# Batch 0's kv sums in one PSUM tile of two banks, and the last output tile in column groups of 320 and 192 instead of 384 and 128

## The chip, the cores and the metric

The kernel runs on one core of one Trainium2 chip. The metric is the device time of one execution in microseconds, the median of several. The time before was 279.4 us. The packed traces keep nanoseconds, while the views round events to 0.01 us and spans to 0.1 us; distances with three decimals below are taken from the packed traces.

## The reference, cut to what matters

```python
def _attn_ref(q, k, v):                      # batch 8, heads 8, sequence 576, head_dim 64
    q_s = softmax(q, axis=-1)                # exp, then divided by the sum over d
    k_s = softmax(k, axis=2)                 # exp, then divided by the sum over the sequence
    kv = np.einsum('bhsd,bhse->bhde', k_s, v)
    return np.einsum('bhsd,bhde->bhse', q_s, kv)

def _moe_ref(x, w_in, w_out):                # 4608 tokens, 512 -> 2048 -> 512
    h = x @ w_in
    g = gelu(h)
    return g @ w_out
```

The code is abridged. The attention output, regrouped by token, is `x`. The softmax of `k` needs no division before the product: the kernel appends a column of ones to `v`, so that the 65th column of kv is the sum, and divides afterwards.

## The kernel before

Nearly all of the time is the two large products (`h_mm`, `y_mm`) on TensorE. The change touches the two ends: the attention of batch 0, which must be done before the first `h_mm`, and the last output tile.

The heads are handled as four pairs (`hp`), two pairs to a half. `kv_mm` sums one half on TensorE, from `ek` (exp of k) and `v_aug` (v in bf16 with its column of ones); `kv_norm` divides it on VectorE into `kvc`, by way of the reciprocals `rec`; `x_mm` then multiplies by the transposed q (`qT`), and an evacuation copies the result to `xT`, the input of `h_mm`. PSUM is the buffer that the matmuls write, and it is divided into banks. Batch 0 has four PSUM banks for its four pairs, two of them from the pool `h`:

```python
def kv_tiles(b):
    if b == 0:
        p = [psum_h.tile([128, 512], FP32, tag="h", name="kv")[:, 0:256] for i in range(2)]
        ps = psum_a.tile([128, 4, 256], FP32, tag="a2", name="kv")   # two banks
        st[b]["kvall"] = ps[:, 0::2]
        p += [ps[:, 0, :], ps[:, 2, :]]
    else:
        ps = psum_a.tile([128, 4, 256], FP32, tag="a2", name="kv")
        st[b]["kvall"] = ps
        p = [ps[:, i, :] for i in place]
    st[b]["kv"] = p
place = [1, 2, 0, 3]

def kv_norm(b, half=None):
    # [cut: which slices; for b == 0 and half == 0 two parts of one pair each]
    for src, dst, m in parts:
        nc.vector.reciprocal(rec[:, 0:m], src[:, :, D])
        nc.vector.tensor_tensor(out=dst, in0=src[:, :, 0:D], in1=[cut: rec, broadcast], op=ALU.mult)

# batch 0, in program order
cast_v(0, 0, nc.scalar); cast_v(0, 1, nc.scalar)
tp_evac(0, 0)
cast_v(0, 2, nc.gpsimd); cast_v(0, 3, nc.gpsimd)
# [cut: two x tiles]
tp_mm(0, 1)                    # second half of the transposes of q
tp_evac(0, 1, "s")
x_tile(0, 2, psum_a, "a")
kv_mm(0, 0)
kv_norm(0, 0)
kv_mm(0, 1)
kv_norm(0, 1)
# [cut: casts of the first weights]
x_mm(0, 0)
x_evac(0, 0, "s"); x_evac(0, 1)
x_mm(0, 1)
x_evac(0, 2, "s"); x_evac(0, 3)
# [cut] then h_phase(0): the first h_mm
```

The last output tile of 128 rows is computed in two column groups, so that the first group's stores are under way while the second is summed:

```python
def y_last():
    for i, (c0, n) in enumerate(((0, 384), (384, 128))):
        ps = psum_y.tile([128, DM], FP32, tag="y")
        for t in range(NDF):                     # 16 matmuls of n columns
            nc.tensor.matmul(ps[:, 0:n], [cut: g], wo_bf[:, t, c0:c0 + n], [cut])
        nc.vector.tensor_copy(out=y_sb[:, 0:n], in_=ps[:, 0:n])
        # [cut] two stores of 64 rows, one issued by SyncE and one by ScalarE
```

The softmax here doesn't subtract the row's maximum and nothing guards it: scores larger than these inputs give would overflow.

Of the kernel before, what the change touches and what calls it, by code (L numbers as in the profile page):

```python
# [8 lines left out]
FP32 = mybir.dt.float32  # L9
# [7 lines left out]
def kernel(  # L17
# [35 lines left out]
    psum_h = ctx.enter_context(tc.tile_pool(name="psum_h", bufs=3, space=bass.MemoryType.PSUM))  # L53
    psum_y = ctx.enter_context(tc.tile_pool(name="psum_y", bufs=2, space=bass.MemoryType.PSUM))
    psum_a = ctx.enter_context(tc.tile_pool(name="psum_a", bufs=1, space=bass.MemoryType.PSUM))
# [12 lines left out]
    kvc = [singles.tile([128, HP, D], BF16, name=f"kvc{b}") for b in range(B)]  # L68
# [12 lines left out]
    st = [dict() for _ in range(B + 1)]  # L81
# [93 lines left out]
    def kv_tiles(b):  # L175


        if b == 0:
            p = [psum_h.tile([128, 512], FP32, tag="h", name="kv")[:, 0:256] for i in range(2)]
            ps = psum_a.tile([128, 4, 256], FP32, tag="a2", name="kv")  # L180
            st[b]["kvall"] = ps[:, 0::2]
            p += [ps[:, 0, :], ps[:, 2, :]]
        else:
            ps = psum_a.tile([128, 4, 256], FP32, tag="a2", name="kv")
            st[b]["kvall"] = ps
            p = [ps[:, i, :] for i in place]
        st[b]["kv"] = p

    place = [1, 2, 0, 3]

# [4 lines left out]
    def kv_mm(b, half):  # L195


        if "kv" not in st[b]:
            kv_tiles(b)
        for n in range(NS):  # L200
            for i in range(2):
                for hh in range(2):
                    hp = 2 * half + i
                    pr = slice(hh * 64, hh * 64 + 64)
                    c = slice((hh ^ i) * 64, (hh ^ i) * 64 + 64)
                    nc.tensor.matmul(  # L206
                        st[b]["kv"][hp][c, 0:D + 1], ek[b % 2][pr, hp, n, :],
                        v_aug[b % 2][pr, hp, n, 0:D + 1], start=(n == 0), stop=(n == NS - 1),
                    )

    def kv_norm(b, half=None):

        ps = st[b]["kvall"]
        if half is None:
            parts = [(ps, kvc[b], 4)]
        elif b == 0 and half == 0:
            parts = [(st[b]["kv"][hp].unsqueeze(1), kvc[b][:, hp:hp + 1], 1) for hp in range(2)]
        elif b == 0:
            parts = [(ps, kvc[b][:, 2:4], 2)]
        else:  # L220
            parts = [(ps[:, 1:3] if half == 0 else ps[:, 0::3], kvc[b][:, 2 * half:2 * half + 2], 2)]
        for src, dst, m in parts:
            rec = small.tile([128, 4], FP32, tag="reck")
            nc.vector.reciprocal(rec[:, 0:m], src[:, :, D])  # L224
            nc.vector.tensor_tensor(  # L225
                out=dst, in0=src[:, :, 0:D],
                in1=rec[:, 0:m].unsqueeze(2).to_broadcast([128, m, D]), op=ALU.mult,
            )

    def kv_step(b):  # L230
        kv_mm(b, 0)
        kv_mm(b, 1)
        kv_norm(b)
# [161 lines left out]
    def y_last():  # L395

        j = J - 1
        for i, (c0, n) in enumerate(((0, 384), (384, 128))):
            ps = psum_y.tile([128, DM], FP32, tag="y")
            for t in range(NDF):  # L400
                nc.tensor.matmul(  # L401
                    ps[:, 0:n], st[B]["g"][:, t, j * 128:(j + 1) * 128],
                    wo_bf[:, t, c0:c0 + n], start=(t == 0), stop=(t == NDF - 1),
                )
            y_sb = moe_sb.tile([128, DM], FP32, tag="y_sb")
            nc.vector.tensor_copy(out=y_sb[:, 0:n], in_=ps[:, 0:n])  # L406
            for b2 in range(2):
                r0 = (2 * j + b2) * S + M
                eng = nc.scalar if b2 else nc.sync
                eng.dma_start(  # L410
                    out=out[r0:r0 + R, c0:c0 + n], in_=y_sb[b2 * R:(b2 + 1) * R, 0:n]
                )

    def y_phase(c, ins):
        for j in range(J - 1 if c == B else J):
            ps = psum_y.tile([128, DM], FP32, tag="y")
            for t in range(NDF):
                y_mm(c, ps, j, t)
                for f in ins.get((j, t), []):
                    f()  # L420
            y_out(c, ps, j)
        if c == B:
            y_last()
# [117 lines left out]
# [5 lines that stand above are left out]
    for dm in range(NDM):  # L546
        cast_wi_dm(0, wi[0], dm, nc.gpsimd)
# [177 lines left out]
```

## Time and profile before

| event, from the timeline of before | us |
|---|---|
| first kv matmul (first half) | 11.55 |
| second kv half released | 12.55 |
| x matmuls of the second half start | 13.63 |
| first h matmul | 13.97 |
| first matmul of the last tile | 270.42 |
| end of the span | 277.5 |

From the first h matmul to the last tile TensorE has no gap to speak of: 256.45 us. This distance is 256.44 to 256.47 us in twelve of the thirteen traces in the fast state, so a kernel's span is the start (up to the first h matmul), plus 256.45, plus the tail (from the last tile on, 7.05 here: the span is 277.471 us before rounding). The profile lines stand in the prediction.

### The profile page before, as it was taken

How to read it: one execution, taken by the hardware profiler on the slowest of the kernel's cores; microseconds unless marked ns; L12 is line 12 of the kernel's file. 1: busy time of each engine (PE TensorE's matmuls, PEld its weight loads, DVE VectorE, ACT ScalarE, POOL GpSimd, SP SyncE). 2: the span in 40 equal slices, each digit the busy share in tenths (PEclk: the TensorE clock that was granted, in tenths of full speed). 3: DMA queues.
4: the chain of work that ended last, by engine and by line, in shares of the span. 5: the costliest groups of instructions: out<-in, count | busy, mean ns of one | idle time of the engine just before them, and what ended most of it. 6: DMA issues, size and time to landing. Idle time of an engine off the chain costs nothing.

```text
span 277.5 us, 4658 instructions
## 1 busy us (share of the span) xinstructions
PE 270.9 (98%) x1966; PEld 125.6 (45%) x1966; DVE 100.8 (36%) x154; ACT 158.9 (57%) x247; POOL 32.5 (12%) x26
## 2 busy tenths in 40 slices
PE   7799999999999999999999999999999999999995
PEld 3344454444444444444444444444444444444443
DVE  2876565319743540263008400751015200120012
ACT  4867686689377717791669246943683363126400
POOL 1520041002020310013000500050005000000000
PEclk9999999999999999999999999999999999999999
DMA  7999999974993249613981189117402500220033
GB/s 258 400 374 427 402 400 404 400 271 116 312 307 64 77 109 297 239 40 94 268 320 38 53 215 398 56 41 193 109 0 78 151 0 0 78 76 0 2 76 77
DMA packets 44980, 50.10 MB, mean 181 GB/s; under 512 B 20384, under 2 KB 29856, under 8 KB 44704
## 3 DMA queue, kind: packets, MB, share of 16 engines
q1 hardware_dynamic: 44560, 49.39, 53.5%
q10 hardware_dynamic: 400, 0.43, 0.5%
q8 instruction: 15, 0.25, 0.4%
q14 instruction: 5, 0.04, 0.1%
HBM read 36.70 MB, written 9.44 MB: 166 GB/s over the span
## 4 chain that ended last, share of the span: by engine, by line
PE 94%; DMA 4%; POOL 0%; DVE 0%; issue 0%; SPq 0%
PE ps L348 44%; PE ps L376 44%; DMA f<-in_v_dram 2%; PE kv L206 2%; PE ps L315 2%; DMA f<-in_q_dram 2%; PE ps L401 1%; PE pair L348 1%; POOL v_aug L169 0%; PE ps L320 0%; PE tp L279 0%; SPq L103 0%; DVE kvc L225 0%; DVE y_sb L406 0%; DVE rec L224 0%
## 5 line engine op out<-in xcount | busy, mean ns | idle before, releaser
L348 PE MATMUL ps<-xT,wi_bf 128*128 128x512 bf16 x568 | 124.9, 379 | 0.0
L376 PE MATMUL ps<-wo_bf,g 128*128 128x512 bf16 x560 | 124.1, 379 | 0.0
L354 ACT ACTIVATE g<-ps 128x512 bf16<-128x512 f32 x142 | 83.5, 598 | 66.8 <-PE ps L348 66.7
L348 PEld LDWEIGHTS <-wi_bf 128*128 128x128 bf16 x576 | 56.2, 98 | 68.0 <-issue 0.8
L376 PEld LDWEIGHTS <-g 128*128 128x128 bf16 x560 | 54.0, 98 | 64.6 <-issue 0.4
L384 DVE COPY y_sb<-ps 128x512 f32<-128x512 f32 x33 | 22.7, 687 | 81.0 <-PE ps L376 80.7
L245 POOL TENSOR_TENSOR e<-e,recq 128x2048 bf16<-128x2048 bf16 (+1 forms) x9 | 25.7, 2855 | 175.9 <-DVE recq L244 141.2
L169 DVE CAST v_aug<-f 128x576 bf16<-128x576 f32 x24 | 16.4, 746 | 48.3 <-DMA f<-in_v_dram 48.3
L243 DVE TENSOR_REDUCE qsum<-e 128x16 f32<-128x1024 bf16 (+1 forms) x13 | 21.1, 1622 | 13.7 <-ACT e L152 13.6
L341 ACT CAST xT<-ps 128x512 bf16<-128x512 f32 x18 | 9.9, 588 | 26.4 <-PE ps L315 15.9
L152 ACT ACTIVATE e<-f 128x512 bf16<-128x512 f32 (+1 forms) x42 | 20.5, 556 | 3.5 <-DMA f<-in_q_dram 3.5
L157 ACT ACTIVATE ek<-f 128x2304 bf16<-128x2304 f32 (+1 forms) x10 | 17.2, 1728 | 0.6 <-DMA f<-in_k_dram 0.5
L339 DVE CAST xT<-ps 128x512 bf16<-128x512 f32 x17 | 11.0, 687 | 17.1 <-PE ps L315 14.1
L79 ACT ACT_TABLE_LOAD x9 | 11.5, 1283 | 2.8 <-issue 2.7
L494 PE MATMUL ps<-zeros 128*128 128x512 f32 x14 | 8.0, 734 | 1.5 <-DVE zeros L520 1.5
L152 ACT ACT_TABLE_LOAD x7 | 9.0, 1283 | 0.1
L453 DVE CAST wi_bf<-w 128x512 bf16<-128x512 f32 x12 | 7.1, 621 | 1.8 <-DMA w<-in_moe_w_in_dram 1.4
L206 PEld LDWEIGHTS <-ek 64*64 64x64 bf16 x576 | 6.4, 105 | 2.2 <-issue 0.6
L206 PE MATMUL kv<-v_aug,ek 64*64 64x65 bf16 x576 | 6.8, 193 | 0.5 <-POOL v_aug L169 0.5
L487 DVE CAST wo_bf<-w 128x2048 bf16<-128x2048 f32 (+1 forms) x5 | 4.5, 907 | 6.1 <-DMA w<-in_moe_w_out_dram 6.1
L245 DVE TENSOR_TENSOR e<-e,recq 128x1024 bf16<-128x1024 bf16 x4 | 6.2, 1544 | 0.1
L315 PE MATMUL ps<-qT,kvc 64*64 64x512 bf16 x62 | 5.4, 390 | 0.3 <-DVE kvc L225 0.3
(40 smaller groups left out, 48.2 us busy)
## 6 DMA issues: line engine op xcount, KB each, us to landing
out_dram<-y_sb SPq DMA_DIRECT2D x32, 256.0 KB, 2.4
f<-in_k_dram SPq DMA_DIRECT2D x6, 1152.0 KB, 9.9
f<-in_v_dram SPq DMA_DIRECT2D x6, 1152.0 KB, 11.7
f<-in_q_dram SPq DMA_DIRECT2D x6, 1024.0 KB, 7.7
w<-in_moe_w_in_dram SPq DMA_DIRECT2D x6, 512.0 KB, 8.6
f<-in_v_dram SPq DMA_DIRECT2D x8, 288.0 KB, 6.5
f<-in_q_dram SPq DMA_DIRECT2D x4, 512.0 KB, 8.9
w<-in_moe_w_out_dram SPq DMA_DIRECT2D x2, 1024.0 KB, 11.4
```

The lines of the kernel that those rows point to most:

```text
L79: nc.scalar.activation(out=scr[:, 1:2], in_=scr[:, 0:1], func=func)
L152: nc.scalar.activation(out=dst[:, i], in_=src[:, u], func=AF.Exp)
L157: nc.scalar.activation(out=ek[b % 2][:, i:i + n], in_=st[b]["kf"][:, i:i + n].rearrange("p x (n d) -> p x n d", n=NS), func=AF.Exp,)
L169: eng.tensor_copy(out=o, in_=i)
L206: nc.tensor.matmul(st[b]["kv"][hp][c, 0:D + 1], ek[b % 2][pr, hp, n, :], v_aug[b % 2][pr, hp, n, 0:D + 1], start=(n == 0), stop=(n == NS - 1),
L243: nc.vector.reduce_sum(out=qsum, in_=eq[:, :, hs, :], axis=AX.X)
L245: eng.tensor_tensor(out=eq[:, :, hs, :], in0=eq[:, :, hs, :], in1=recq.unsqueeze(3).to_broadcast([128, J, w, D]), op=ALU.mult,)
L339: nc.vector.tensor_copy(out=st[b]["xT"][:, hp, :], in_=ps)
L348: nc.tensor.matmul(ps, wi_bf[:, dm, t * 128:(t + 1) * 128], st[c]["xT"][:, dm, :], start=(dm == 0), stop=(dm == NDM - 1),)
L354: nc.scalar.activation(out=st[c]["g"][:, t, :], in_=ps, func=AF.Gelu)
L376: nc.tensor.matmul(ps, st[c]["g"][:, t, j * 128:(j + 1) * 128], wo_bf[:, t, :], start=(t == 0), stop=(t == NDF - 1),)
L384: nc.vector.tensor_copy(out=y_sb, in_=ps)
```

## The change

The intent of part 1 is to hold batch 0's kv as all other batches hold theirs: fewer VectorE instructions, and two buffers of the pool `h` free. That of part 2 is a better balance between the two stores of the last tile.

```diff
     def kv_tiles(b):
-        if b == 0:
-            p = [psum_h.tile([128, 512], FP32, tag="h", name="kv")[:, 0:256] for i in range(2)]
-            ps = psum_a.tile([128, 4, 256], FP32, tag="a2", name="kv")
-            st[b]["kvall"] = ps[:, 0::2]
-            p += [ps[:, 0, :], ps[:, 2, :]]
-        else:
-            ps = psum_a.tile([128, 4, 256], FP32, tag="a2", name="kv")
-            st[b]["kvall"] = ps
-            p = [ps[:, i, :] for i in place]
-        st[b]["kv"] = p
+        ps = psum_a.tile([128, 4, 256], FP32, tag="a2", name="kv")
+        st[b]["kvall"] = ps
+        st[b]["kv"] = [ps[:, i, :] for i in place]
@@ kv_norm
-        elif b == 0 and half == 0:
-            parts = [(st[b]["kv"][hp].unsqueeze(1), kvc[b][:, hp:hp + 1], 1) for hp in range(2)]
-        elif b == 0:
-            parts = [(ps, kvc[b][:, 2:4], 2)]
@@ y_last
-        for i, (c0, n) in enumerate(((0, 384), (384, 128))):
+        for i, (c0, n) in enumerate(((0, 320), (320, 192))):
```

Both halves of kv now lie in the same two banks. In the built program the first weight load of the second kv half has a new wait for VectorE, called the guard below: it keeps TensorE from writing the banks while VectorE still reads the first half there. The x matmuls of the first half have lost their wait. Nothing else moves but the shapes.

## The prediction

> **What bounds the kernel now.** I read the page's busy table and slices first, then the chain that ended last in order of time, then the timeline of the two ends, which are all that the change touches.
>
> ```profile
> span 277.5 us, 4658 instructions
> PE 270.9 (98%) x1966; PEld 125.6 (45%) x1966; DVE 100.8 (36%) x154; ACT 158.9 (57%) x247; POOL 32.5 (12%) x26
> PE   7799999999999999999999999999999999999995
> ```
>
> TensorE is busy 98% of the span, and only the first two slices and the last have gaps: 14 us at the start, where the data arrive, and the last 3.4 us, where the last output leaves. Time can be won or lost only there; the timed median of 279.4 us adds a constant 1.9 us to the span.
>
> The chain of waits in the order of time shows the start:
>
> ```profile
> 11.83 0.68 POOL v_aug L169
> 12.51 0.04 issue
> 12.55 0.50 PE kv L206 x34
> 13.05 0.02 issue
> 13.08 0.18 DVE rec L224
> 13.26 0.02 issue
> 13.28 0.30 DVE kvc L225
> 13.58 0.04 issue
> 13.63 0.41 PE ps L315 x4
> 14.04 6.15 PE ps L348 x28
> ```
>
> The second half of kv waits for GpSimd's last cast of v (it ends at 12.51), is normalised, and feeds the second half of the x matmuls. The timeline of the same stretch shows what lies beside it:
>
> ```profile
> 12.08 0.17 DVE L224 RECIPROCAL rec<-kv 128x1 f32<-128x1 f32 x1 [0.61 <-PE kv L206]
> 12.28 0.23 DVE L225 TENSOR_TENSOR kvc<-kv,rec 128x64 bf16<-128x64 f32 x1
> 12.42 0.16 DVE L224 RECIPROCAL rec<-kv 128x1 f32<-128x1 f32 x1
> 12.61 0.23 DVE L225 TENSOR_TENSOR kvc<-kv,rec 128x64 bf16<-128x64 f32 x1
> 12.84 0.46 PE L315 MATMUL ps<-qT,kvc 64*64 64x512 bf16 x4
> 13.34 0.59 ACT L341 CAST xT<-ps 128x512 bf16<-128x512 f32 x1 [0.67 <-PE ps L315]
> 13.97 7.51 PE L348 MATMUL ps<-xT,wi_bf 128*128 128x512 bf16 x34
> ```
>
> The first h matmul, which starts the unbroken stream, is at 13.97: ScalarE's evacuation of the first x tile ends at 13.93. So two branches meet there: the x matmuls of the first half (12.84, evacuated from 13.34), and those of the second half, which are ahead of it in TensorE's order and start at 13.63.
>
> The timeline of the end:
>
> ```profile
> 273.23 0.56 DVE L406 COPY y_sb<-ps 128x384 f32<-128x384 f32 x1 [1.91 <-PE ps L401]
> 273.81 1.11 SPq L410 DMA_DIRECT2D out_dram<-y_sb  x2
> 273.82 1.38 ACTq L410 DMA_DIRECT2D out_dram<-y_sb  x2
> 274.12 0.29 DVE L406 COPY y_sb<-ps 128x128 f32<-128x128 f32 x1 [0.33 <-PE ps L401]
> ```
>
> Matmul, copy of 128 columns (0.29), two stores, the wait for their landing: the second column group alone sets the end. The stores of the first group land at about 275.9 and 276.2 (issued at 273.8, 2.1 and 2.4 us to landing), those of the second at about 276.4 and 276.6 (issued at 274.43 and 274.46, 2.0 and 2.1 us).
>
> **What the Trainium skill says.** "PSUM — Partial Sum Buffer", section "PSUM bank collisions raise a hardware error", says that two engines may not touch the same bank and quadrant of partitions at once, even at other addresses, and tells the author to guard PSUM by bank. That bears on the first part: one tile of two banks puts the first half of kv (being read) and the second half (being written) in the same banks. The trace before cannot show this, since the halves are in four different banks there. "TensorE: Matmul & The Clock Gate", section "Back-to-back issue gap", gives N/2.4 + 2.5 ns for one matmul after another at the full clock, with a caution that weight loads can make small ones slower (81 ns at N=128). Here the 16 matmuls of 384 columns and 16 of 128 fill 270.42 to 274.10: 16 x 162.5 = 2.60 us, and then 0.86 us for 15 gaps, 57 ns each, before a last one of 0.219. So the trace agrees with the formula and not with the caution. "DMA: Bandwidth & Descriptors", section "Anatomy of one DMA — SWDGE (gpsimd) path", says that about 2 us of a transfer is fixed, most of it the receipt of the write. These stores use the other descriptor path, yet agree: 32 KB takes 2.0 to 2.1 us and 96 KB 2.1 to 2.4.
>
> **Part 1, kv of batch 0.** In place of two tiles of the h pool and one of two banks there is one tile of two banks, with the heads placed so that each half is one slice across both banks. Instructions: the matmuls are the same; four VectorE instructions become two. What they were: 0.17 + 0.23 + 0.16 + 0.23, running from 12.08 to 12.84. The pair that replaces them has the shape of the second half's pair in this trace (0.17 from 13.08, 0.29 from 13.28, end 13.57, thus 0.49 after its start). So the first half is normalised by 12.08 + 0.49 = 12.57, 0.27 us earlier.
>
> That gain does not reach the path. The built program shows a wait moved: the first weight load of the second kv half now waits for VectorE, and the x matmuls no longer do. This is the bank guard, against the normalisation of the first half. So the second kv half starts not at 12.55 (GpSimd) but at 12.57 plus the 0.05 us that a hand-over from VectorE to TensorE takes here (13.57 to 13.62): 12.62, which is +0.07. Also, of its 36 matmuls two ran ahead before, in the group that started at 11.55 (38 in that row, 34 in the later one); now all 36 wait, two more at 8.3 ns (the starts of the 34 spread over 12.55 to 12.83): +0.02. The two branches:
> - second half: kv ends near 13.11 for 13.02, x matmuls start at 13.72 for 13.63, first h matmul could issue about 0.22 us after them, at 13.94. That is below 13.97, so this branch had slack and does not set it.
> - first half: x matmuls start once the kv matmuls have issued, 12.62 + 0.02 + 36 x 0.0083 = 12.94 for 12.84. Before, the second of them also waited for the second normalisation (12.84 + 0.05 = 12.89), so the loss is 0.05 to 0.10. ScalarE's evacuation and the first h matmul move with it: 13.97 becomes about 14.04.
>
> The later evacuations move by 0.09 at most; the h group has 0.43 us of work on the first x tile and again on the second, so they stay hidden. The h pool's buffers turn two places earlier, and nothing waits for them. **Part 1: +0.07 us.**
>
> **Part 2, the last output tile.** The columns are the same 512 x 16, the matmuls the same 32. Working from the gap formula: before 16 x 162.5 + 15 x 57 + 219 = 3.67 us; after 16 x 135.8 + 15 x 82.5 + 246 (379 ns at 512 columns and 219 at 128 in the table by form give 0.417 ns a column) = 3.66. TensorE ends at 274.10 either way. The copy behind it has 64 more columns: 558 ns for 384 and 291 for 128 give 1.04 ns a column, so 0.36 for 0.29: +0.07. The stores go out at about 274.50 for 274.43. They carry 48 KB each for 32, which from 2.0 at 32 KB and 2.1 at 96 is +0.03 on SyncE's, and 2.1 to 2.4, +0.07, on ScalarE's. Against that, the first group now ends 16 x 26.7 ns = 0.43 us sooner and its copy is 0.07 shorter, so its stores (80 KB each) go out at 273.31, and their data are gone before the second group's begin. Before, the DMA view shows the engines at 7 to 9 tenths without a break from 274.9 to 276.1 for both pairs, so the second pair queued behind the first for part of its time; 96 KB at the 205 GB/s of that stretch need 0.47 us from about 275.6, thus to 276.07. I take the relief as -0.12. **Part 2: +0.07 + 0.05 - 0.12 = 0.00 us.**
>
> **Sum:** +0.07 us: 279.40 becomes 279.47.
>
> **Rivals.**
> 1. Part 1 gains: the x matmuls of the first half start up to 0.27 us sooner because kvc is there sooner. Against it: they stand behind the second kv half in TensorE's order, and that waited for GpSimd until 12.55 anyway. Only if the guard were free would this be worth anything: 0.0 to -0.05 us.
> 2. The tail gains: the two store pairs overlapped in the DMA engines, and now do not. If most of the landing time of the second pair was queueing, the end moves by -0.2 us: 279.27. For it: the unbroken DMA stretch. Against it: 2.0 to 2.1 us to landing is no longer than the 2.0 to 2.4 of other stores with nothing beside them.
> 3. The tail loses: landing grows with bytes and nothing was queued: +0.07 copy and up to +0.1 landing, with part 1 about 279.65.
> 4. The pauses before 14 us grow enough to lower the granted clock (1.00 in every stretch before). The pause that grows is 0.5 us before kv's second half, so I give this 2%; it could cost around 1 us.
>
> **Range and chances.** The sums are hundredths, of either sign; three timed runs spread over 0.05 us, and the profiled run took 279.26, so sessions may differ by 0.15. I take 279.2 to 279.75. Two per cent is 5.6 us, and nothing here is a tenth of that: within 2% has 0.98.
>
> **What would show it.** Right: the second kv half starts about 12.62 and its idle time is put down to VectorE's kvc; the first h matmul near 14.04; TensorE's last matmul ends as late after the start of the last tile as before (3.66 us); the copies take 0.49 and 0.36; no overlap of the store pairs. Wrong: kv's second half still released by GpSimd at 12.55; a first h matmul at or before 13.97; 192-column matmuls spaced by more than 83 ns; an end of the data after 276.2; a clock under 1.00.

## The result, and the profile after

The changed kernel took 279.57 us (six runs, 279.46 to 279.75), the kernel before 279.39 us (six runs, 279.25 to 279.44). The ratio is 1.0007 with a 95% interval of 0.9995 to 1.002: the same within 2%, and by time alone not even shown to be slower. Ratios are computed as the mean time of one kernel's fast runs over that of the other's of the same rounds, so they are not quite the ratio of the medians.

The chain of waits of the changed kernel in order of time (start, duration, what; both in us) shows the new order of events:

```profile
9.24 1.72 DVE e L234
...
11.70 0.45 PE kv L199 x34
...
12.38 0.30 DVE kvc L214
12.69 0.04 issue
12.73 0.52 PE kv L199 x34
...
13.48 0.30 DVE kvc L214
13.78 0.04 issue
13.82 0.41 PE ps L304 x4
14.23 5.93 PE ps L337 x27
```

GpSimd's cast of v has left the chain. The second kv half (12.73) follows the first half's normalisation (which ends at 12.67), that follows the first kv half, and that follows the q path (`e` is q's normalisation). The timeline of the same stretch says the same in the brackets (idle time before, and what ended it):

```profile
12.73 0.48 PE L199 MATMUL kv<-v_aug,ek 64*64 64x65 bf16 x36 [0.61 <-DVE kvc L214]
13.04 0.39 PE L304 MATMUL ps<-qT,kvc 64*64 64x512 bf16 x4
...
13.47 0.58 ACT L330 CAST xT<-ps 128x512 bf16<-128x512 f32 x1 [0.72 <-PE ps L304]
...
13.82 0.41 PE L304 MATMUL ps<-qT,kvc 64*64 64x512 bf16 x4 [0.40 <-DVE kvc L214]
...
14.17 0.39 PE L337 MATMUL ps<-xT,wi_bf 128*128 128x512 bf16 x1
```

The first h matmul is at 14.17, against 13.97 before: +0.19 us before rounding. But the first kv half also began later, at 11.63 against 11.55: in this execution the data of q landed 0.09 us later (the chain's first transfer lasts 4.28 us for 4.19), which the change cannot have done. Measured from the first kv matmul, the first h matmul is 2.425 us later in the kernel before and 2.535 us later in the changed one: **+0.11 us is the change's**, and 0.08 chance.

The timeline of the tail:

```profile
270.63 3.66 PE L390 MATMUL ps<-wo_bf,g 128*128 128x320 bf16 x32
...
273.00 0.49 DVE L395 COPY y_sb<-ps 128x320 f32<-128x320 f32 x1 [1.48 <-PE ps L390]
273.52 1.65 SPq L399 DMA_DIRECT2D out_dram<-y_sb  x2
273.53 1.69 ACTq L399 DMA_DIRECT2D out_dram<-y_sb  x2
274.32 0.36 DVE L395 COPY y_sb<-ps 128x192 f32<-128x192 f32 x1 [0.83 <-PE ps L390]
```

TensorE needs 3.66 us for the tile in both kernels; the last copy takes 0.36 us for 0.29. The span ends at 277.732, thus 7.103 us after the tile's start, for 7.047 before: **+0.06 us**. The transfers' busy share in 40 slices from 273 to 278 us, first before, then after, shows that the two pairs of stores no longer overlap:

```profile
DMA  5799930000000003999997684000000000000000
```

```profile
DMA  9969988202000598994000277771000000000000
```

### The profile page after: what moved, and what is told of

Its sections match the earlier page's. It is cut to its first block, busy times and chain, and to the rows that moved or that the text cites. A ratio compares the mean times of both kernels' runs of the same rounds, so it can differ in the third digit from the quotient of the medians.

```text
span 277.7 us, 4656 instructions
## 1 busy us (share of the span) xinstructions
PE 270.6 (97%) x1966; PEld 125.9 (45%) x1966; DVE 100.2 (36%) x152; ACT 158.8 (57%) x247; POOL 32.4 (12%) x26
## 4 chain that ended last, share of the span: by engine, by line
PE 94%; DVE 2%; DMA 2%; ACT 0%; issue 0%
PE ps L337 44%; PE ps L365 44%; PE kv L199 2%; PE ps L304 2%; DMA f<-in_q_dram 2%; PE ps L390 1%; DVE qsum L232 1%; PE pair L337 1%; DVE e L234 1%; ACT e L152 0%; PE ps L309 0%; PE tp L268 0%; DVE kvc L214 0%; PE ps L248 0%; DVE recq L233 0%
```

## The experiments

All outputs are right. The column "kv to h" is the distance from the first kv matmul to the first h matmul, "tail" that from the last tile's first matmul to the end of the span, both in us from the one trace of the run, taken from the nanoseconds of the packed trace. (Spans rounded to 0.1 us, from which some of the expectations worked out their tails, are too coarse for differences of 0.06 us.) In the kernels that move the first kv half, the first distance means something else and is left out; the time of the first h matmul stands in its place.

| run | time, us | before beside it | ratio (95%) | kv to h | tail |
|---|---|---|---|---|---|
| before, first trace | | 279.39 | | 2.425 | 7.047 |
| changed, first trace | 279.57 | 279.39 | 1.0007 (0.9995 to 1.002) | 2.535 | 7.103 |
| null_before | 279.4 | 279.43 | 0.9999 (0.9985 to 1.0012) | | |
| after_again | 279.53 | 279.43 | 1.0005 (0.9992 to 1.0017) | 2.531 | 7.115 |
| kv_only | 279.59 | 279.43 | 1.0005 (0.9991 to 1.0019) | 2.532 | 7.107 |
| cols_only | 279.49 | 279.43 | 1.0002 (0.999 to 1.0015) | 2.423 | 7.119 |
| norm_twice | 279.87 | 279.41 | 1.0015 (1.0 to 1.0031) | 2.932 | 7.030 |
| kv_first | 279.4 | 279.41 | 0.9996 (0.9984 to 1.0009) | h at 13.84 | 7.033 |
| kv_first_before | 279.17 | 279.41 | 0.9992 (0.9979 to 1.0004) | h at 13.89 | 7.045 |
| kv_first_before2 | 279.21 | 279.45 | 0.999 (0.9977 to 1.0002) | h at 13.88 | 7.034 |
| balanced | 279.41 | 279.41 | 1.0001 (0.9988 to 1.0013) | h at 14.04 | 7.026 |
| kv_first_whole | 279.41 | 279.45 | 0.9995 (0.9981 to 1.0009) | h at 13.96 | 7.106 |
| cols_256 | 279.75 | 279.45 | 1.0009 (0.9995 to 1.0022) | 2.423 | 7.240 |
| cols_448 | 280.15 | 279.45 | 1.0024 (1.001 to 1.0038) | 2.422 | 7.676 |

**The kernel before against itself** (no edit).

> A control: the kernel before, timed against itself. All theories: ratio 1.000, within 0.0005. Its first h matmul should lie near 13.97 us; where it lies elsewhere, the distance is the jitter of the data's arrival between executions, and no single trace may be read below that.

Four of its five runs were 279.36 to 279.41. The fifth, the profiled one, took 409.57 us at a mean granted clock of 0.659; it is not compared with anything, and its trace can't show the jitter of the data's arrival. Other traces can: cols_only, cols_256 and cols_448 below leave the start of the kernel untouched, and their first h matmuls are at 14.11, 14.33 and 14.18 for 13.97. So the absolute start moves by 0.35 us from one execution to another, three times what the change costs, while kv to h is 2.422 to 2.425 in all four. The interval shows what the timing can resolve: some 0.13%, or 0.35 us.

**The changed kernel again** (no edit).

> The changed kernel again, for a closer interval. My theory (the bank guard puts the second kv half behind the first half's normalisation, and that behind the q path) expects 1.0003 to 1.0009. A rival, that the +0.18 us of the first comparison is chance of the data's arrival, expects 1.0000 to 1.0002. In the trace the first matmul of the second kv half should again be released by VectorE's kvc and not by GpSimd's cast.

The ratio is in the range of the theory, but its interval holds 1.000, so the time alone does not refute the rival. The trace does: the second kv half is again released by `kvc`, and kv to h is 2.531 us, 0.11 more than before.

**Part 1 alone.**

```diff
-        for i, (c0, n) in enumerate(((0, 320), (320, 192))):
+        for i, (c0, n) in enumerate(((0, 384), (384, 128))):      # on the changed kernel
```

> Part 1 alone (columns 384 and 128 kept). My theory: all of the loss is here, so the same ratio as the whole change, 1.0003 to 1.0009, and the first h matmul 0.07 to 0.20 us later than in the control. Rival (the loss is in the last tile's longer copy and stores): 1.0000.

The distance from kv to h is 2.532 us, that of the whole change. So the start is part 1's. (Its tail is 7.107, longer than the other six with 384 and 128 columns, 7.026 to 7.047: both of its last stores took 0.05 to 0.08 us longer to land, for which no cause is known.) "All of the loss" was too much: part 2 has a share, as follows.

**Part 2 alone.**

```diff
-        for i, (c0, n) in enumerate(((0, 384), (384, 128))):
+        for i, (c0, n) in enumerate(((0, 320), (320, 192))):      # on the kernel before
```

> Part 2 alone (kv as before). My theory: the last copy costs 0.07 us more and the stores of 192 columns land as soon as those of 128 because nothing is queued before them, so 1.0000 within 0.0003, and from the last matmul's end to the span's end 3.4 us as before. Rival (the tail loses by copy and bytes): 1.0003 to 1.0006. Rival (the tail gains because the store pairs no longer overlap): 0.9993.

The start is the old one (2.423), the tail 7.119 us, longer than any of the seven with 384 and 128 columns. This trace also settles what released the first h matmul before the change (timeline of cols_only):

```profile
11.68 0.51 PE L206 MATMUL kv<-v_aug,ek 64*64 64x65 bf16 x38
...
12.40 0.47 PE L206 MATMUL kv<-v_aug,ek 64*64 64x65 bf16 x34 [0.21 <-POOL v_aug L169]
...
13.47 1.07 ACT L341 CAST xT<-ps 128x512 bf16<-128x512 f32 x2 [0.67 <-PE ps L315]
...
14.11 0.59 PE L348 MATMUL ps<-xT,wi_bf 128*128 128x512 bf16 x2 [0.22 <-ACT xT L341]
```

Here GpSimd's cast was early: the second kv half began 0.72 us after the first, against 1.00 in the first trace of before. The first h matmul still came 2.423 us after the first kv half. (In cols_256 and cols_448 the second half did not wait at all, and it was 2.423 and 2.422.) So the cast, which the chain of waits of the kernel before had named, was not what the start hung on in these executions; in the first trace it was level with the path through the first half's normalisation, x matmuls and ScalarE's evacuation.

**The suspected wait, made longer.**

```diff
     kv_norm(0, 0)
+    kv_norm(0, 0)          # on part 1 alone; same result
```

> Part 1 alone with the first half's normalisation done twice, to the same place (0.5 us of VectorE more, result unchanged). My theory, revised by the first traces: in the changed kernel the second kv half waits for this normalisation, and the first h matmul stands behind the x matmuls that hang on the second half; so the whole 0.5 us appears: second kv half 1.6 us after the first half's start for 1.1, first h matmul 3.0 us after it for 2.53, time +0.5 us on part 1 alone (ratio to before 1.0022). Rival (GpSimd's cast or TensorE's order sets the second half): no change in the second half's start, and +0.0 to +0.1 us.

Timeline of norm_twice:

```profile
12.42 0.29 DVE L214 TENSOR_TENSOR kvc<-kv,rec 128x128 bf16<-128x128 f32 x1
...
12.82 0.29 DVE L214 TENSOR_TENSOR kvc<-kv,rec 128x128 bf16<-128x128 f32 x1
13.17 0.48 PE L199 MATMUL kv<-v_aug,ek 64*64 64x65 bf16 x36 [1.02 <-DVE kvc L214]
...
14.61 0.60 PE L337 MATMUL ps<-xT,wi_bf 128*128 128x512 bf16 x2
```

The second pair of instructions ended 0.40 us after the first (the second reciprocal overlaps), the second kv half began 1.50 us after the first for 1.10, and kv to h grew by the same 0.40, from 2.532 to 2.932. The whole delay reaches the first h matmul. The ratio to before is 1.0015, less than the 1.0022 expected. The theory had the mechanism; its 0.5 us was too much by the overlap. The rival's 0.0 to 0.1 is excluded by the trace.

**The wait, opened in time.** The first kv half does not need the second half of the transposes, which stands ahead of it.

```diff
-    tp_mm(0, 1)
-    tp_evac(0, 1, "s")
-    x_tile(0, 2, psum_a, "a")
     kv_mm(0, 0)
+    tp_mm(0, 1)
     kv_norm(0, 0)
+    tp_evac(0, 1, "s")
+    x_tile(0, 2, psum_a, "a")     # on part 1 alone
```

> Part 1 alone with the first kv half moved in TensorE's order ahead of the second half of the transposes (which it does not need). Its normalisation is then done near 12.2 us, before GpSimd's cast ends, so the guard is open when it is asked for. My theory: the second kv half is released by GpSimd again (12.3 to 12.55), first h matmul 13.75 to 13.97, ratio 0.9990 to 1.0000, so 0.2 us better than part 1 alone. Rival (the merged tile is slow for another reason, e.g. both halves in the same banks): still 0.1 us slower than before.

Timeline of kv_first:

```profile
10.97 1.39 POOL L169 CAST v_aug<-f 128x576 bf16<-128x576 f32 x2 [0.91 <-DMA f<-in_v_dram]
...
11.87 0.29 DVE L214 TENSOR_TENSOR kvc<-kv,rec 128x128 bf16<-128x128 f32 x1
...
12.22 0.68 PE L199 MATMUL kv<-v_aug,ek 64*64 64x65 bf16 x36
...
13.49 0.41 PE L304 MATMUL ps<-qT,kvc 64*64 64x512 bf16 x4 [0.38 <-DVE kvc L214]
```

The wait opens at 12.2, before GpSimd's cast ends at 12.37: two of the 36 matmuls start at 12.22, and the 34 that need that cast from 12.42 on. The h matmuls start at 13.84 for 14.25 in part 1 alone, although q landed 0.12 us later here (5.21 for 5.09), and the median is 279.4 for 279.59, in different sessions. So the loss of part 1 lies in this wait, and goes when the wait is open before it is asked for.

**The same move on the kernel before.**

> The same move on the kernel before, which has no guard. My theory: within 0.05 us of kv_first, since with the guard open the two layouts differ in two VectorE instructions that are off the path. Rival (the guard costs even where it is open, or the merged normalisation is worth its 0.27 us once the path runs over it): the two differ by 0.1 to 0.3 us.

The first h matmul is at 13.89, 0.05 us from kv_first, as the theory had it. What is left is the arrival of v: measured from the end of GpSimd's last cast, the first h matmul comes 1.467 us later in kv_first and 1.465 us later here. The times differ by 0.23 us (279.17 and 279.4), but not by their intervals, and their traces' spans are 277.4 and 277.3, the other way round. The traces say the layouts are level once the wait is open; the times do not contradict that and do not show it.

**An attempt to beat both.** To kv_first_before, the casts of v dealt out in turn.

```diff
     cast_v(0, 0, nc.scalar)
-    cast_v(0, 1, nc.scalar)
+    cast_v(0, 1, nc.gpsimd)
     tp_evac(0, 0)
-    cast_v(0, 2, nc.gpsimd)
+    cast_v(0, 2, nc.scalar)
     cast_v(0, 3, nc.gpsimd)
```

> An attempt to beat both: kv_first_before with the four casts of v dealt out alternately to ScalarE and GpSimd in place of two and two in a row, so that the last cast ends near 11.7 us for 12.5. My theory (the path to the first h matmul is v's last cast, second kv half, normalisation, x matmuls): first h matmul near 13.7, ratio 0.9990 (279.15 us). Rival (the weights' cast on GpSimd, or q's path, is as late): 13.9 or later, ratio 0.9997 to 1.0000.

Missed. Timeline of balanced:

```profile
10.40 0.98 POOL L169 CAST v_aug<-f 128x576 bf16<-128x576 f32 x1 [0.62 <-DMA f<-in_v_dram]
...
11.43 0.47 PE L206 MATMUL kv<-v_aug,ek 64*64 64x65 bf16 x34 [0.55 <-POOL v_aug L169]
11.81 0.67 POOL L169 CAST v_aug<-f 128x576 bf16<-128x576 f32 x1 [0.43 <-DMA f<-in_v_dram]
...
12.49 1.01 ACT L270 COPY qT<-ps 128x1024 bf16<-128x1024 bf16 x1 [0.76 <-PE ps L259]
...
13.40 1.24 ACT L341 CAST xT<-ps 128x512 bf16<-128x512 f32 x2
```

In this trace the last part of v does not arrive before 11.8 us, so GpSimd's cast of it (0.67 us) cannot end before 12.48. What had looked like a queue on GpSimd was the arrival of the data. With the usual 1.47 us after that cast the first h matmul would come at 13.94. It came at 14.04, 0.05 us after ScalarE's first evacuation (13.40, 0.59 us long), which stood directly behind ScalarE's copy of `qT`. That copy was late because the first kv half, and with it the transposes behind it, now waited for GpSimd until 11.43. So the last 0.10 us lay on q's path, one of the rival's two causes.

**The whole change with the move.** The edit of kv_first on the changed kernel.

> The whole change (one kv tile, 320 and 192 columns) with the first kv half moved ahead of the second half of the transposes. The guard is then open before it is asked for: first h matmul 13.80 to 13.95, tail as in the changed kernel, so 0.2 us better than the changed kernel and 0.05 to 0.1 better than before: ratio 0.9995 to 1.0000. Rival (the guard was not the cause): 1.0005 like the changed kernel.

The first h matmul is at 13.96, 0.01 us outside the range, and the median 279.41 us, 0.1 better than the changed kernel. But the profiled run (279.70) was the slowest of five that spread from 279.17, and it shows what made it slow. Its chain of waits, further on:

```profile
11.08 9.31 DMA w<-in_moe_w_in_dram
20.39 0.02 issue
20.41 0.64 DVE wi_bf L442
21.05 0.04 issue
21.09 0.61 PE ps L337 x2
```

A part of the first weights landed at 20.39 us (the cast that follows it began at 19.6 in the first traces of both kernels), and TensorE waited for it: from the first h matmul to the last tile this trace has 256.85 us in place of 256.45. In the other twelve traces that part landed at 19.4 to 20.0 us and TensorE did not wait. Since the first h matmul of this trace is no earlier than before's (13.96 and 13.97), it was the late landing, and not an early start, that made the wait; that an earlier start meets this bound more often is plausible but not shown, and how often it happens is not known from one trace.

**The move on the kernel before, once more**, as the version that may beat both.

> The kernel before with only that move, again, as the version that may beat both: first h matmul 13.80 to 13.95 against 13.97 to 14.1 without the move, ratio 0.9990 to 0.9997. Rival (its 0.9992 was chance of the data's arrival): 1.0000.

The first h matmul is at 13.88, and all five runs (279.12 to 279.31) lie below all nine of the kernel before beside them (279.33 to 279.65); on the first chip the two ranges overlap (279.06 to 279.49, 279.28 to 279.69). On two chips the ratio came out 0.9992 and 0.999, each interval just reaching 1.000. It is the best version tried, by some 0.2 us, and this 0.1% is at the edge of what the runs can show. The traces say where it comes from: the first h matmul again follows v's last cast by 1.465 us, and in cols_only, cols_256 and cols_448, which lack the move, it came 0.29, 0.43 and 0.37 us later than that cast plus 1.467.

**The tail, one step further.**

```diff
-        for i, (c0, n) in enumerate(((0, 384), (384, 128))):
+        for i, (c0, n) in enumerate(((0, 256), (256, 256))):      # on the kernel before
```

> Kernel before, last tile in 256 and 256 columns: one step further in the direction of part 2. From the start of the last tile's matmuls to the span's end the six traces with 384 and 128 have 7.01 to 7.09 us, the three with 320 and 192 7.07 to 7.15. My theory now (the end pays the longer last copy and the bytes, and gets nothing back from the earlier first stores): last copy 0.42 us, and 7.2 us in this stretch. Theory of the prediction (relief of the queue pays for the copy): 7.05 again.

The tail is 7.240 us, the last copy 0.42 us: copy and bytes are paid, and the earlier first stores give nothing back on the last store.

**The tail, one step the other way.**

```diff
-        for i, (c0, n) in enumerate(((0, 384), (384, 128))):
+        for i, (c0, n) in enumerate(((0, 448), (448, 64))):       # on the kernel before
```

> Kernel before, last tile in 448 and 64 columns: one step the other way. If only the last copy and its bytes count, the stretch falls by 0.07 to 0.1 us, to 6.95, provided that 64-column matmuls follow each other in 64/2.4 + 2.5 = 29 ns. If small matmuls are held to about 57 ns or more by their weight loads, TensorE's part grows by 16 x 28 ns = 0.45 us and the stretch is 7.4 us or more. If the queue of the first stores counts, the second pair lands later than 2.1 us after its issue.

The tail is 7.676 us, 0.63 more than before, mostly for a reason that none of the three had. The timeline of cols_448, and the landing of its stores (KB each, us from issue to landing):

```profile
270.62 3.66 PE L401 MATMUL ps<-wo_bf,g 128*128 128x448 bf16 x32
...
273.85 0.76 DVE L406 COPY y_sb<-ps 128x448 f32<-128x448 f32 x2 [2.33 <-PE ps L401]
274.50 1.11 SPq L410 DMA_DIRECT2D out_dram<-y_sb  x2
274.51 1.39 ACTq L410 DMA_DIRECT2D out_dram<-y_sb  x2
```

```profile
out_dram<-y_sb SPq DMA_DIRECT2D x1, 16.0 KB, 2.2
out_dram<-y_sb ACTq DMA_DIRECT2D x1, 16.0 KB, 2.3
```

TensorE still needs 3.66 us (so 64-column matmuls are not held up by their weight loads: that rival falls). But the first group's copy runs from 273.85 for 0.62 us, past TensorE's end at 274.28, and the second copy waits for it. Then the second stores wait for the issue of the first: they go out at 275.1, some 0.5 us after their copy ended near 274.6. Last, they land 2.2 and 2.3 us after issue, later than the larger stores of 32 KB (2.0 and 2.1), as the third theory expected of a queue. The split has a best place between two losses; 384 and 128 is the best of the four tried.

## Why the prediction was right or wrong

The time came out inside the range, 0.10 us above the number. The range, 279.2 to 279.75, would also have held no change or a gain of 0.2 us, so this alone says little for the steps:

- **The moved wait: right.** The second kv half was to start 1.07 us after the first kv matmul (12.62 less 11.55); it started 1.10 after (12.73 less 11.63), released by `kvc`. norm_twice and kv_first show that this wait is the cause.
- **The second-half branch "had slack": wrong.** This is the step that failed. It took 0.22 us from the start of that half's x matmuls to the first h matmul, which gave this branch 0.12 us of slack (13.63 + 0.22 for 13.97). The traces have 0.342 or 0.343 us after the change, in norm_twice and in all kernels that move the first kv half but balanced, and 0.348 before. So the branch was level with ScalarE's evacuation before, to 6 ns, and the whole delay of the second half counts: 0.11 us in three traces, for the 0.07 in the sum. The sign was right partly by luck: the 0.07 came from the other branch, which did not set the h matmul.
- **The first-half branch: about right.** ScalarE's evacuation came 1.79 us after the first kv matmul before and 1.84 after: +0.05, the lower end of what was given. It no longer sets the h matmul.
- **TensorE's part of the last tile and the copies: right.** 3.66 us, 0.49 and 0.36.
- **The relief of the queue, -0.12 us: wrong in size.** The pairs no longer overlap, as was said, but the last pair lands 1.9 and 2.1 us after issue for 2.0 and 2.1: SyncE's store gained a tenth and ScalarE's, which ends last, nothing. An estimate: stores of 64 KB without overlap (cols_256) landed 0.07 us later than those of 48 KB, so 16 KB more cost about 0.07 us on either store; the relief was then about 0.17 us on SyncE's store and only 0.05 on ScalarE's. The seven fast tails with 384 and 128 average 7.046 us, the four with 320 and 192 7.111: +0.065, about what the longer copy costs, for a sum of 0.00.
- **The rivals.** The first (part 1 gains) and the second (the tail gains) fall. The third (the tail loses) holds for the copy's 0.07 us, without the 0.1 for landing. The fourth did not occur: the clock was 1.00 in the profiled runs of both kernels; the one slow run was the kernel before's.
- **Its signs of being wrong.** One came true: the last stores' data were to end by 276.2 and ended at 276.49, or 276.28 counted from the same start of the last tile. Three readings were also off: the busy share of the DMA engines, read as 7 to 9 tenths without a break, falls to 5 in slices of 0.06 us; TensorE's last matmul ended at 274.08, not 274.10, so the gaps at 128 columns are 56 ns and not 57; and the "constant 1.9 us" took the median less the span of another execution: for the profiled one it is 279.26 less 277.47, or 1.8.

Together, 0.11 + 0.065 = 0.175 us, for measured differences of medians of 0.18 and 0.10 us; the predicted 0.07 is less than half of it, since both mis-sized terms were reliefs that hardly reached the end. That these two make up the time is shown in the traces; in the times alone no single part is separable from noise.

What stays open: how often the weights' arrival takes back an earlier start, and why the landing of the last stores shifts as it does by tenths between SyncE and ScalarE.

## What to carry to other kernels

Merging buffers saves instructions, but where a reader and the next writer then share a PSUM bank, the writer waits for the reader: look in the built program for which wait moved, and hand the first reader its data earlier before you merge. A chain of waits names one path; where two are level, an execution in which one of them happened to be early shows which counts. And a split of a last tile is a balance between the last copy, the issue of the stores and their landing, so try a step on each side before moving it.

## What the Trainium skill lacked or had wrong

- "PSUM — Partial Sum Buffer", section "PSUM bank collisions raise a hardware error", tells the author to guard by bank but not what the guard costs: here 0.11 us at the first h matmul, with 0.055 us from VectorE's end (12.674) to TensorE's start (12.729). That two engines would collide was not tried.
- "TensorE: Matmul & The Clock Gate", section "Back-to-back issue gap", warns of 81 ns a matmul at 128 columns when each has its weight load, and keeps the simple formula for isolated matmuls. Here, with a weight load for each, the matmuls started 56 ns apart at 128 columns and 29 at 64 (cols_448): the simple formula held in both. At 512 columns the section has 131 ns; the h matmuls started 216 ns apart (34 of them in 7.51 us). Another section of the page, "Wait — 56ns, not 53.3ns?", has 55.6 and 215.7 ns back to back, which agrees with what was measured here.
- The same page, section "Part 3: Packing small matmuls — row/col tiling", does not say how soon a full-array matmul can follow packed ones, and "TensorEngine Tiling (Array Packing)", section "Key Properties", has only that a change of tiling mode drains TensorE: here 0.342 us after the start of four of 64x64 with 512 columns, which last 0.40 each. Whether this is that drain was not tested.
- "DMA: Bandwidth & Descriptors", section "Anatomy of one DMA — SWDGE (gpsimd) path", gives about 2 us fixed; stores of 16 to 112 KB here landed in 1.9 to 2.6 us. It does not have that, of two stores of equal size issued within 0.1 us, ScalarE's landed later than SyncE's each time (2.4 and 2.1 us at 96 KB, 2.3 and 2.0 at 80); whether by the queue, the order of issue or the rows was not tested.
- "TensorE: Matmul & The Clock Gate" has no state like that of the control's slow run, the program's one core at a mean granted clock of 0.659: 0.65 in every stretch from 10 us on, and 407.8 us for a span of 277.5.
